# Three separate output banks, a second bank for one Gelu input, and a searched order in an RWKV + Gelu-MLP kernel

## The chip, the cores and the metric

The kernel runs on one core of a Trainium2 chip. The metric is the device time of one execution in microseconds (us), given as the median of several runs. Before the change it is 481.47 us, the median of three runs (480.07, 481.47 and 481.57).

## What is computed

Two stages follow each other in float32. The first is an RWKV recurrence for 4 batches, 8 heads, 768 time steps and head width 48; the second is a Gelu MLP on the 3072 resulting tokens of width 384, with hidden width 2048.

```
cur   = (u * k_t) outer v_t
y_t   = r_t . (state + cur)          # per batch and head; state is 48 x 48
state = w * state + k_t outer v_t    # w is per head and channel, 0.85 to 0.95
x     = y, laid out as 3072 tokens x 384
out   = gelu(x @ w_in) @ w_out       # exact (erf) Gelu
```

## The kernel before, in words

**Tiling.** The 768 time steps are cut into 6 chunks of 128. The 8 heads form 4 pairs, so there are 24 groups (chunk, pair). Inside a group the recurrence is written with powers of w as matrix products: scores of r against k, a masked copy of them, a product with v, and a product with the carried state. The first four groups (chunk 0) have no state to read and are built by `first_group`; the others by `group`. The result of a group is copied out of PSUM as a rounded high half and a low half (`keep`), and together four groups give the x of 512 tokens.

**The MLP** runs over 6 chunks x 16 slices of the hidden width = 96 steps m. In step m `moe1` computes the hidden slice by 9 matmuls (three products: high weights x high x, low weights x high x, high weights x low x, each over three blocks of 128 rows) into the one PSUM bank `Hp`. ScalarE reads `Hp` twice with Gelu (`gh`, rounded, and `gf`, full), and VectorE forms their difference `gl`. `moe2` then adds 9 matmuls into the three output banks, which collect 16 steps. So the next step's first matmul into `Hp` has to wait until both Gelus of the step before have read it. A step is 18 matmuls of 512 columns.

**Weights.** Each of the 16 slices is loaded once as 64-bit numbers (`w_load`, three raw buffers) and turned into a high and a low half by five instructions (`w_split`): two on ScalarE (L395, L398), one add on VectorE (L400), a rounding copy to `wh` on ScalarE (L404), and a subtraction to `wl` on VectorE (L407). All 16 are made during chunk 0 of the MLP.

**PSUM.** The eight banks are `A` (two banks, one tile), `YU` (banks Y and U, one tile), `Hp`, `OO` (output banks 0 and 1, one tile) and `O2`. The chunk-0 groups borrow them: even groups write their scores to `A` and their y to `O2`; odd groups write scores to `OO` and y to `Y`. Two transposes (`flip`) use `U`.

**Order.** All work is given to a planner, the class `Plan`: engine, estimated ns, due time, what it reads and writes by name. `run` carries due times back through the users, `play` then simulates the engines (a free engine takes the ready operation with the smallest due time), and emits each instruction at the moment its turn comes. All DMAs are issued by one queue, SP, in that order, and every engine executes its instructions strictly in that order. Where the simulated TensorE would idle early in the kernel, `play` puts in a dummy matmul ("heat", L305). Semaphores are added afterwards by the framework from what each instruction really touches in a tile.

**The end.** The last chunk's output leaves in four parts (L763 to L774). Then every engine reaches `tc.If` (L909): a general path for values of w outside a range, skipped here; its transfers are issued by ScalarE.

Of the kernel before, what the change touches and what calls it, by code (L numbers as in the profile page):

```python
# [9 lines left out]
F32 = mybir.dt.float32  # L10
# [35 lines left out]
SWAP_DUE = 50000  # L46
ROUND = "a"
# [4 lines left out]
PRODUCT = ("d", "d", "d", "d")  # L52
# [3 lines left out]
class Plan:  # L56
# [11 lines left out]
    def __init__(self, after):  # L68
        self.after = after
        self.ops, self.writer, self.readers, self.reads, self.writes = [], {}, {}, [], []  # L70
        self.heats, self.heat_ns, self.heat_room, self.heat_from, self.heat_to = {}, 0, 0, None, None

# [27 lines left out]
    def run(self):  # L100
        self.users = [[] for _ in self.ops]
        due = [o[2] for o in self.ops]
        for n in reversed(range(len(self.ops))):
# [3 lines left out]
        self.play(due)  # L107

    def play(self, due):

        ops = self.ops
        left = [len(o[4]) for o in ops]
# [4 lines left out]
        clear, unread, held, heating = {}, {}, None, False  # L117
# [3 lines left out]
        for _ in ops:  # L121
# [23 lines left out]
            while e == "pe" and heating:  # L145
# [5 lines left out]
                self.heats[b]()  # L151
# [6 lines left out]
            _, ns, _, fn, _, port = ops[n]  # L158
            if e == "sp":
                free[e] = start + self.DMA_GAP  # L160
                queued = bus - start - self.DMA_LEAD
                bus = max(bus, start + self.DMA_LEAD) + ns / self.DMA_RATES[start >= self.DMA_EARLY]
                end = bus + self.DMA_FIXED + self.DMA_SPREAD * (queued > self.DMA_QUEUED)
# [3 lines left out]
            ins = fn()  # L167
            if port:
                locked[e] = end
                if e == "dve":  # L170
                    held = ins
                elif held is not None:
                    self.after(ins, held, "port")
# [9 lines left out]
            for m in self.users[n]:  # L183
                ready[m] = max(ready[m], end + self.lag(n, m))
                left[m] -= 1
                if not left[m]:
                    heapq.heappush(waiting[ops[m][0]], (ready[m], m))


def rwkv_gelu_mlp(tc, rkT, rkv, wuT, uN, wmlp, r, k, vT, w, u, out):  # L190
    nc = tc.nc
    with ExitStack() as ctx:
# [110 lines left out]

        def heat(dst):
            nc.tensor.matmul(dst, lhsT=zeros[:, 0:128], rhs=zeros, start=True, stop=True)  # L305

        def warm_up():
            for n in range(HEATS):
                heat((A + O + [Y, U])[n % 7])

# [5 lines left out]
        plan.heats, plan.heat_ns, plan.heat_room = {("H",): lambda: heat(Hp), ("U", "Y"): lambda: heat(U)}, HEAT_NS, HEAT_ROOM  # L316
        plan.heat_from = add("pe", 430 * HEATS, 10, warm_up, r=["zeros"], w=["H", "A0", "A1", "O0", "O1", "O2", "Y", "U"])
# [34 lines left out]
        def flip(src):  # L352
            for p in range(NP):
                nc.tensor.transpose(U[:, p * 128:p * 128 + LP], src(p), ident[:LP, :LP])

        def flipped(dst):
            return lambda: nc.scalar.copy(out=dst, in_=U.rearrange("s (p j x) -> s p j x", p=NP, x=64)[:, :, :, :D])

        add("act", 1700, LATER, state_powers, r=["P"], w=["WKs"])
        add("pe", 560, LATER, lambda: flip(lambda p: WKs[:, p, :]), r=["WKs", "ident"], w=["U"])  # L360
        add("act", 400, LATER, flipped(WN), r=["U"], w=["WN"])
# [11 lines left out]
        add("pe", 560, LATER, lambda: flip(lambda p: E[:, p, 1].rearrange("l h i -> l (h i)")), r=EVERY + ["ident"], w=["U"])  # L373
        add("act", 400, LATER, flipped(WN2), r=["U"], w=["WN2"])
# [70 lines left out]
        def first_group(gi, at, XX, XB, y, YB):  # L445
# [8 lines left out]
            for i, e in enumerate(halves):  # L454
# [7 lines left out]
                    r=["P", f"W{p}", f"T{gi}"], w=[f"{TR}{b}" for b in range(bs.start, bs.stop)], port=True)  # L462
            me = PRODUCT[gi]
            mul = nc.vector.tensor_tensor if me == "d" else nc.gpsimd.tensor_tensor
            add("dve" if me == "d" else "pool", dve(512) if me == "d" else pool(512), LATER, lambda: mul(
                out=RK[gi], in0=T[gi][:LP, 0, :, ::-1], in1=T[gi][:LP, 1], op=ALU.mult), r=[f"T{gi}"], w=[f"RK{gi}"], port=True)

            def sum_pairs():
                for b in range(NB):
# [4 lines left out]
            add("pe", 1070, LATER, sum_pairs, r=[f"RK{gi}", "w_sb"], w=["H"])  # L474
            add("act", 110, LATER, lambda: nc.scalar.copy(
                out=sums.rearrange("s (b j) -> s b j", j=2),
                in_=Hp[:, 0:NB * WIDE].rearrange("s (b x) -> s b x", x=WIDE)[:, :, 0:2]), r=["H"], w=[CS])
# [215 lines left out]
        def product1(x, j, n, ks=range(3), start=False, stop=False):  # L693
            wt, a = ((wh, 0), (wl, 0), (wh, 1))[n]
            for k_ in ks:
                nc.tensor.matmul(Hp, lhsT=wt[j][:, 0, k_ * 128:(k_ + 1) * 128], rhs=x[:, a, k_, :],  # L696
# [9 lines left out]
        def moe1(m, at):  # L706
# [6 lines left out]
            n1 = 2 * j  # L713
            if m == 0:
                gaps0 = lambda k_: gaps[2 * k_:2 * k_ + 2]
                for k_ in range(3):
                    first = add("pe", 3 * MM, at + k_, lambda k_=k_: [
                        product1(x, j, n, (k_,), k_ == 0 and n == 0, k_ == 2 and n == 2) for n in range(3)],
                        r=["wh0", "wl0"] + xr("h", (k_,)) + xr("l", (k_,)) + gaps0(k_), w=["H"])
                    plan.heat_to = plan.heat_to or first  # L720
            else:
                for n in range(3):
                    add("pe", 3 * MM, at + n, lambda n=n: product1(x, j, n, start=n == 0, stop=n == 2),
                        r=[f"{('wh', 'wl', 'wh')[n]}{n1}"] + xr("hhl"[n]) + gaps, w=["H"])
            add("act", 480, LATER, lambda: nc.scalar.activation(out=high, in_=Hp, func=AF.Gelu, scale=256.0), r=["H"], w=[GH])  # L725
# [274 lines left out]
```

## Time and profile before

| | |
|---|---|
| median of three runs | 481.47 us |
| the profiled execution | 480.38 us, of which 478.6 us from first to last instruction |
| TensorE matmuls busy | 469.6 us, 98% |
| VectorE, ScalarE, GpSimd busy | 229.0, 181.8, 67.6 us |
| granted TensorE clock | 0.998 of full speed |
| moved by DMA | 46.60 MB, of which 5 to 30 us runs at about 400 GB/s |

PE is TensorE's matmuls, PEld its weight loads, DVE is VectorE, ACT ScalarE, POOL GpSimd, SP the queue that issues the DMAs. L606 is line 606 of the kernel. A matmul's own duration overlaps with its neighbours, so the distance between starts is what counts for the time: a 512-column matmul takes one slot of about 0.233 us. Idle time of an engine that others do not wait for costs nothing.

### The profile page before, as it was taken

The page shows a single profiled execution, that of the slowest core. Times are in us where ns is not written, and L with a number is a line of the kernel's source. Part 1 is how long each engine was busy: PE and PEld are TensorE (multiplying, and loading weights), DVE is VectorE, ACT ScalarE, POOL GpSimd, SP SyncE. Part 2 cuts the span into 40 slices and gives each one's busy share as a digit, 9 for nine tenths or more (in the row PEclk, how much of TensorE's full clock was granted, in tenths as well). Part 3 has the DMA queues.
Part 4 walks back from the last instruction along what each step waited for, and adds up shares of the span by engine and source line. Part 5 has one row for each costly group of instructions (what it writes and reads, how often), then busy time and mean ns, then how long its engine had stood idle before and what let it go on. Part 6 is the DMA issues. An engine that isn't in the chain of part 4 may idle for free.

```text
span 478.6 us, 10284 instructions
## 1 busy us (share of the span) xinstructions
PE 469.6 (98%) x4525; PEld 378.4 (79%) x4525; DVE 229.0 (48%) x345; ACT 181.8 (38%) x333; POOL 67.6 (14%) x91
## 2 busy tenths in 40 slices
PE   8989999999999999999999999999999999999995
PEld 6767788888888787888888888888888887888874
DVE  7989989754354356153543543534434311211111
ACT  9898988232222223232223222223322223322221
POOL 1332021221120222010202202202102000000000
PEclk9999999999999999999999999999999999999999
DMA  8978682314033034031231230321402000100002
GB/s 299 349 305 293 238 296 70 114 54 161 13 95 104 3 113 153 1 105 43 64 105 67 95 102 4 105 59 46 162 29 77 14 0 12 66 1 1 1 0 71
DMA packets 15426, 46.60 MB, mean 97 GB/s; under 512 B 3664, under 2 KB 4048, under 8 KB 15376
## 3 DMA queue, kind: packets, MB, share of 16 engines
q1 hardware_dynamic: 15376, 45.88, 28.9%
q8 instruction: 37, 0.61, 0.5%
q14 instruction: 13, 0.11, 0.1%
HBM read 38.73 MB, written 4.72 MB: 91 GB/s over the span
## 4 chain that ended last, share of the span: by engine, by line
PE 89%; ACT 4%; DMA 4%; DVE 1%; issue 0%; ACTq 0%
PE Hp L696 41%; PE O L737 40%; PE Y L606 2%; DMA E<-W 2%; PE Y L634 2%; PE A L614 2%; DMA raw<-in_wmlp_dram 1%; PE A L623 1%; PE Y L737 1%; ACT wa L395 1%; ACT wh L404 0%; DVE wb L400 0%; ACT W L344 0%; ACT Sa L530 0%; ACT gh L725 0%
## 5 line engine op out<-in xcount | busy, mean ns | idle before, releaser
L696 PE MATMUL Hp<-xx,wh 128*128 128x512 f32 x576 | 168.5, 400 | 0.0
L727 DVE TENSOR_TENSOR gl<-gf,gh 128x512 fp32r<-128x512 f32 x93 | 66.8, 719 | 170.3 <-ACT gf L726 170.0
L725 ACT ACTIVATE gh<-Hp 128x512 fp32r<-128x512 f32 x93 | 55.6, 598 | 219.1 <-PE Hp L696 219.1
L696 PEld LDWEIGHTS Hp<-xx,wh 128*128 128x128 f32 x576 | 105.6, 188 | 25.5 <-ACT gf L726 0.6
L696 PE MATMUL Hp<-xx,wl 128*128 128x512 f32 x288 | 83.0, 395 | 0.0
L737 PE MATMUL O<-gh,wh 128*128 128x512 f32 (+1 forms) x279 | 79.1, 391 | 1.6 <-ACT gh L725 1.5
L737 PE MATMUL O<-gh,wl 128*128 128x512 f32 (+1 forms) x279 | 79.0, 391 | 0.0
L737 PE MATMUL O<-gl,wh 128*128 128x512 f32 (+1 forms) x279 | 78.9, 390 | 0.0
L696 PEld LDWEIGHTS Hp<-xx,wl 128*128 128x128 f32 x288 | 54.1, 188 | 12.9
L737 PEld LDWEIGHTS O<-gh,wh 128*128 128x128 f32 x279 | 52.1, 188 | 15.0 <-ACT gh L725 2.9
L737 PEld LDWEIGHTS O<-gh,wl 128*128 128x128 f32 x279 | 51.6, 188 | 11.7
L737 PEld LDWEIGHTS O<-gl,wh 128*128 128x128 f32 x279 | 51.4, 188 | 11.5 <-issue 0.4
L726 ACT ACTIVATE gf<-Hp 128x512 f32<-128x512 f32 x96 | 56.9, 593 | 0.0
L561 POOL TENSOR_TENSOR Nb<-Nb 128x384 f32<-128x384 f32 x20 | 20.3, 1017 | 125.4 <-DMA Nb<-in_rkv_dram 81.3
L558 DVE TENSOR_TENSOR Tb<-Tb,E 112x1024 f32<-112x1024 f32 x20 | 24.8, 1240 | 2.6 <-DMA Tb<-in_rkT_dram 2.5
L663 DVE SCALAR_TENSOR_TENSOR Sb<-Sa,E,A 48x192 f32<-48x192 f32 x40 | 16.5, 413 | 18.0 <-PE A L623 17.3
L433 ACT CAST xx<-Y 112x512 fp32r<-112x512 f32 (+1 forms) x17 | 10.0, 586 | 39.3 <-PE Y L634 39.3
L564 POOL TENSOR_TENSOR Nb<-Nb,WN 128x384 f32<-128x384 f32 x20 | 20.3, 1017 | 22.9 <-DVE wl L407 14.3
L567 POOL TENSOR_TENSOR Nb<-Nb,u_sb 128x384 f32<-128x384 f32 x20 | 20.3, 1013 | 15.4 <-DVE gl L727 13.6
L570 DVE TENSOR_REDUCE cs<-Nb 128x8 f32<-128x384 f32 x20 | 11.0, 552 | 18.1 <-POOL Nb L567 15.8
L644 POOL MEMSET done<- 1x1 f32 x19 | 1.7, 89 | 125.4 <-PE Y L606 125.4
L670 DVE COPY_PREDICATED Am<-past,A 128x512 f32<-128x512 uint32 x20 | 14.9, 747 | 7.0 <-PE A L623 6.8
(112 smaller groups left out, 376.3 us busy)
## 6 DMA issues: line engine op xcount, KB each, us to landing
raw<-in_wmlp_dram SPq DMA_DIRECT2D x16, 767.8 KB, 6.5
Nb<-in_rkv_dram SPq DMA_DIRECT2D x20, 576.0 KB, 5.5
Tb<-in_rkT_dram SPq DMA_DIRECT2D x20, 512.0 KB, 4.2
out_dram<-raw SPq DMA_DIRECT2D x5, 768.0 KB, 3.6
T<-in_rkT_dram SPq DMA_DIRECT2D x4, 512.0 KB, 5.3
xx<-x SPq DMA_DIRECT2D x30, 64.0 KB, 4.1
N<-in_rkv_dram SPq DMA_DIRECT2D x4, 384.0 KB, 7.3
out_dram<-raw SPq DMA_DIRECT2D x2, 256.0 KB, 2.5
```

Of the source, the lines that this page charges most:

```text
L558: add("dve", 1140, LATER, lambda: nc.vector.tensor_tensor(out=flat, in0=flat, in1=E[:, p, 0].rearrange("l h i -> l (h i)").unsqueeze(1).to ...
L561: add("pool", pool(DM), LATER, lambda: nc.gpsimd.tensor_tensor(out=n[:, 0], in0=n[:, 0], in1=n[:, 1], op=ALU.mult), r=[NK], w=[NR])
L564: add("pool", pool(DM), LATER, lambda: nc.gpsimd.tensor_tensor(out=kn, in0=kn, in1=WN2[:, p].rearrange("s j d -> s (j d)").unsqueeze(1).to ...
L567: add("pool", pool(DM), LATER, lambda: nc.gpsimd.tensor_tensor(out=n[:, 0], in0=n[:, 0], in1=u_sb[:, p, :].unsqueeze(1).to_broadcast([C, N ...
L570: add("dve", 465, LATER, lambda: nc.vector.tensor_reduce(out=sums, in_=n[:, 0].rearrange("s b (j d) -> s (b j) d", d=D), axis=AX.X, op=ALU ...
L663: add("dve", 430, at, lambda l=l, x=x: nc.vector.scalar_tensor_tensor(out=out[quarter(1 - x)], in0=src[l], scalar=E[l, p, 1, h, 32:33], in ...
L670: add("dve", 625, LATER, lambda: nc.vector.copy_predicated(out=am, mask=past2.bitcast(U32).unsqueeze(1).unsqueeze(1).to_broadcast([C, 2, N ...
L696: nc.tensor.matmul(Hp, lhsT=wt[j][:, 0, k_ * 128:(k_ + 1) * 128], rhs=x[:, a, k_, :], start=start and k_ == ks[0], stop=stop and k_ == ks[-1])
L725: add("act", 480, LATER, lambda: nc.scalar.activation(out=high, in_=Hp, func=AF.Gelu, scale=256.0), r=["H"], w=[GH])
L726: add("act", 480, LATER, lambda: nc.scalar.activation(out=gf, in_=Hp, func=AF.Gelu, scale=256.0), r=["H"], w=["gf"])
L727: add("dve", dve(512), LATER, lambda: nc.vector.tensor_tensor(out=low, in0=gf, in1=high.bitcast(F32), op=ALU.subtract), r=["gf", GH], w=[G ...
L737: nc.tensor.matmul(dst[:, a:b], lhsT=wt[j][:, 1, d * 128:(d + 1) * 128], rhs=gt[:, a:b], start=(j == 0 and n == 0), stop=(j == NJ - 1 and ...
```

## The change

Six edits.

1. The output banks 0, 1 and 2 become three tiles of one bank each, in place of one tile of two banks and one of one. Chunk-0 odd groups now write their scores to `YU` and their y to bank O1; the two transposes and one of the dummy-matmul targets move from `U` to O0.
2. The hidden slice of step 1 (and of no other step) is computed into output bank O2 and read by its Gelus from there. The output products of step 0 are split into those for banks 0 and 1 and those for bank 2.
3. `Plan.run` makes 2000 trials: it disturbs the due times of 1 to 4 operations, plays the order up to an operation called the judge (the last hidden product of step 21), replays that order four times with durations disturbed by 4%, and keeps the disturbance where the sum of the four judged times is not larger. The kept due times then give the whole order.
4. The first group's keys and receptances (512 KB) come in two transfers, for batches 0 and 1 and for batches 2 and 3; the product of the two (`RK`) and its sums are split in the same way for this group.
5. In the general path, the transfers move from ScalarE's to GpSimd's queue.
6. `PRODUCT` (all "d", VectorE) goes away.

```diff
+SEARCH, REPLAYS, HEAT, SEED = 2000, 4, 0.0, 2
...
     def run(self):
...
+        noise = [[1 + chance.gauss(0, 0.04) for _ in self.ops] for _ in range(REPLAYS)]
+        judged = lambda order: sum(self.replay(order, x) for x in noise)
+        order = self.play(due, self.judge)
+        end, near = judged(order), [n for n in order if isinstance(n, int) and self.ops[n][0] != "do"]
+        best, kept = end, due
+        for i in range(SEARCH):
+            other = list(due)
+            for n in chance.sample(near, chance.choice((1, 1, 2, 4))):
+                other[n] += chance.gauss(0, chance.choice((1500, 4000, 10000)))
+            got = judged(self.play(other, self.judge))
+            if got <= end + HEAT * REPLAYS * (1 - i / SEARCH) * chance.random():
+                end, due = got, other
+            if end < best:
+                best, kept = end, due
+        due = kept
+        self.issue(self.play(due))
...
-        OO = psp.tile([128, 2, 512], F32, name="O")
-        O = [OO[:, i] for i in range(2)] + [psp.tile([128, 512], F32, name="O2")]
+        O = [psp.tile([128, 512], F32, name=f"O{i}") for i in range(3)]
...
+        halves_of = lambda gi: ((0, 1), (2, 3)) if gi == 0 else (range(NB),)
+
         def load_group(gi, at, r=()):
             s = slot(gi)
-            dma(C * 4096, at, lambda: nc.sync.dma_start(T[s], rkT[gi]), r=r, w=[f"T{s}"])
+            for bs in halves_of(gi):
+                dma(C * 1024 * len(bs), at, lambda bs=slice(bs[0], bs[-1] + 1): nc.sync.dma_start(
+                    T[s][:, :, bs], rkT[gi, :, :, bs]), r=r, w=[f"T{s}{b}" for b in bs] if gi < NP else [f"T{s}"])
...
+            for bs in halves_of(gi):
+                sl, Tn, Rn = slice(bs[0], bs[-1] + 1), [f"T{gi}{b}" for b in bs], [f"RK{gi}{b}" for b in bs]
+                add("dve", dve(128 * len(bs)), LATER, lambda sl=sl: nc.vector.tensor_tensor(
+                    out=RK[gi][:, sl], in0=T[gi][:LP, 0, sl, ::-1], in1=T[gi][:LP, 1, sl], op=ALU.mult),
+                    r=Tn, w=Rn, port=True)
+                add("pe", 268 * len(bs), LATER, lambda bs=bs: sum_pairs(bs), r=Rn + ["w_sb"], w=[f"H{b}" for b in bs])
...
+            dst, H_ = (O[2], "O2") if m == 1 else (Hp, "H")
...
+                    last = add("pe", 3 * MM, at + n, lambda n=n: product1(x, j, n, start=n == 0, stop=n == 2, dst=dst),
+                        r=[f"{('wh', 'wl', 'wh')[n]}{n1}"] + xr("hhl"[n]) + gaps, w=[H_])
+                if m == NJ + 5:
+                    plan.judge = last
...
-            if m < NSTEP - 2:
+            if m == 0:
+                for which in ((0, 1), (2,)):
+                    for n in range(3):
+                        go(m, n, which, at + n)
+            elif m < NSTEP - 2:
...
-            first_group(gi, LATER, AA if even else OO, ["A0", "A1"] if even else ["O0", "O1"],
-                        O[2] if even else Y, "O2" if even else "Y")
+            first_group(gi, LATER, AA if even else YU, ["A0", "A1"] if even else ["Y", "U"],
+                        O[2] if even else O[1], "O2" if even else "O1")
...
-                nc.scalar.dma_start(wb[l, h // 2], w[h].partition_broadcast(D))
+                nc.gpsimd.dma_start(wb[l, h // 2], w[h].partition_broadcast(D))
```

`play` no longer emits; it returns the order, and `issue` emits it. `replay` walks a given order with the disturbed durations and returns the end of the judge.

## Rows read from the trace of the kernel before

**Rows 1.** The page, part 1: busy us (share of the span) xinstructions.
```profile
PE 469.6 (98%) x4525; PEld 378.4 (79%) x4525; DVE 229.0 (48%) x345; ACT 181.8 (38%) x333; POOL 67.6 (14%) x91
```

**Rows 2.** Waits of PE from 20 us on: us in total, times, longest.
```profile
PE O L737 <- ACT gh L725: 1.5, 1, 1.5
PE O L737 <- ACT raw L771: 0.7, 1, 0.7
```

**Rows 3.** Windows: length, busy us by engine, PE clock, DMA share, GB/s.
```profile
5.00:10.00 5.00, 4.92 (x38) 3.61 (x38) 4.56 (x8) 4.90 (x20) 0.00 (x0) 1.00 1.03 409
...
30.00:35.00 5.00, 5.00 (x81) 3.66 (x79) 3.35 (x3) 4.94 (x8) 1.99 (x2) 1.00 0.50 208
40.00:50.00 10.00, 9.88 (x139) 7.75 (x130) 9.89 (x16) 9.89 (x14) 0.09 (x1) 1.00 0.87 302
```

**Rows 4.** Timeline of the last ten us: start, us, engine, line, operation.
```profile
469.91 0.63 PE L737 MATMUL O<-xx,wh 128*128 128x512 f32 x2
470.57 0.60 ACT L771 ACTIVATE raw<-O 128x512 f32<-128x512 f32 x1 [1.93 <-PE O L737]
...
471.22 0.50 PE L737 MATMUL O<-xx,wl 128*128 128x512 f32 x1 [0.69 <-ACT raw L771]
...
474.67 0.52 SPq L774 DMA_DIRECT2D out_dram<-Nb  x1
```

**Rows 5.** Line 909, SP's joins behind the skipped path: ns min/median/max, first to last.
```profile
L909 SPq EVENT_SEMAPHORE  x8: 17/17/17, 475.7 to 477.3; - x8
```

**Rows 6.** Timeline of PE: step 0's last products, its first output products, two later triples.
```profile
26.85 0.40 PE L696 MATMUL Hp<-xx,wh 128*128 128x512 f32 x1
28.73 0.96 PE L737 MATMUL O<-gh,wh 128*128 128x512 f32 x3 [1.48 <-ACT gh L725]
...
46.69 0.86 PE L696 MATMUL Hp<-xx,wl 128*128 128x512 f32 x3
47.39 0.86 PE L696 MATMUL Hp<-xx,wh 128*128 128x512 f32 x3
```

**Rows 7.** Timeline around that wait: weights of step 1, group 4's scaling, first Gelu.
```profile
25.58 1.65 DVE L558 TENSOR_TENSOR Tb<-Tb,E 112x1024 f32<-112x1024 f32 x1
...
26.21 0.81 ACT L404 CAST wh<-wb 128x768 fp32r<-128x768 f32 x1
...
27.16 0.94 DVE L407 TENSOR_TENSOR wl<-wb,wh 128x768 fp32r<-128x768 f32 x1
...
28.09 0.58 ACT L725 ACTIVATE gh<-Hp 128x512 fp32r<-128x512 f32 x1
...
29.80 1.22 DVE L558 TENSOR_TENSOR Tb<-Tb,E 112x1024 f32<-112x1024 f32 x1
```

**Rows 8.** Timeline of the start: key loads, first product, scaled halves, first scores.
```profile
1.28 1.36 SPq L264 DMA_DIRECT2D T<-in_rkT_dram  x3
...
5.44 0.69 DVE L465 TENSOR_TENSOR RK<-T 112x512 f32<-112x512 f32 x1 [0.76 <-DMA T<-in_rkT_dram]
...
7.33 1.22 DVE L459 TENSOR_TENSOR Ts<-T,W 112x512 f32<-112x512 f32 x2
...
8.14 1.18 PE L484 MATMUL A<-Ts 64*128 64x128 f32 x16
```

**Rows 9.** The page, part 6: DMA issues, KB each, median us to landing.
```profile
xx<-x SPq DMA_DIRECT2D x30, 64.0 KB, 4.1
...
out_dram<-raw SPq DMA_DIRECT2D x2, 256.0 KB, 2.5
```

**Rows 10.** Timeline of 41 to 43 us: step 3's low weights and their use.
```profile
41.29 0.95 DVE L407 TENSOR_TENSOR wl<-wb,wh 128x768 fp32r<-128x768 f32 x1
...
42.80 0.86 PE L696 MATMUL Hp<-xx,wl 128*128 128x512 f32 x3
```

**Rows 11.** Timeline before step 32: the last x pieces of chunk 2, its first products.
```profile
170.32 1.63 SPq L441 DMA_DIRECT2D xx<-x  x2
...
179.31 0.97 PE L696 MATMUL Hp<-xx,wh 128*128 128x512 f32 x3
```

More of the change, by code (lines that the diff above doesn't have):

```diff
@@ L100, in run @@
     def run(self):
+        count = len(self.ops)
         self.users = [[] for _ in self.ops]
         due = [o[2] for o in self.ops]
-        for n in reversed(range(len(self.ops))):
+        for n in reversed(range(count)):
             for d in self.ops[n][4]:
@@ new lines, in land, with replay @@
+    def land(self, start, bus, ns, slow=1.0):
+        queued = bus - start - self.DMA_LEAD
+        bus = max(bus, start + self.DMA_LEAD) + ns * slow / self.DMA_RATES[start >= self.DMA_EARLY]
+        return bus + self.DMA_FIXED + self.DMA_SPREAD * (queued > self.DMA_QUEUED), bus
+    def replay(self, order, slow):
+        ops, ends = self.ops, {}
+        free = {e: 800.0 for e in self.LAG}
+        bus, locked, lanes = 0.0, {"dve": 0.0, "pool": 0.0}, [0.0] * self.DMA_LANES
+        for n in order:
+            if not isinstance(n, int):
+                free["pe"] += self.heat_ns
+                continue
+            e, ns, _, _, deps, port = ops[n]
+            start = free[e]
+            for d in deps:
+                start = max(start, ends[d] + self.lag(d, n))
+            if port:
+                start = max(start, locked["pool" if e == "dve" else "dve"])
+            if e == "sp":
+                start = max(start, lanes[0])
+                free[e] = start + self.DMA_GAP
+                ends[n], bus = self.land(start, bus, ns, slow[n])
+                lanes = lanes[1:] + [ends[n]]
+            else:
+                free[e] = ends[n] = start + ns * (slow[n] if e != "pe" else 1.0)
+            if port:
+                locked[e] = ends[n]
+        return ends[n]
@@ L111, in play, with issue @@
+    def issue(self, order):
+        held = None
+        for n in order:
+            if not isinstance(n, int):
+                self.heats[n]()
+                continue
+            ins = self.ops[n][3]()
+            if self.ops[n][5]:
+                if self.ops[n][0] == "dve":
+                    held = ins
+                elif held is not None:
+                    self.after(ins, held, "port")
+    def play(self, due, stop=None):
         ops = self.ops
+        order = []
         left = [len(o[4]) for o in ops]
@@ L187, in play @@
                     heapq.heappush(waiting[ops[m][0]], (ready[m], m))
+            if n == stop:
+                break
+        return order
 def rwkv_gelu_mlp(tc, rkT, rkv, wuT, uN, wmlp, r, k, vT, w, u, out):
@@ L301, in rwkv_gelu_mlp @@
         add("act", 520, LATER, spread_ones, r=["ident", "zeros"], w=["spread"])
+        HB = [f"H{b}" for b in range(NB)]
         def heat(dst):
@@ L461, in first_group, with sum_pairs @@
                         in1=W[:, p, 0:C].unsqueeze(1).unsqueeze(1).to_broadcast([LP, 2, nb, C]), op=ALU.mult),
[L462 to L469, printed above, removed]
+                    r=["P", f"W{p}"] + [f"T{gi}{b}" for b in range(bs.start, bs.stop)],
+                    w=[f"{TR}{b}" for b in range(bs.start, bs.stop)], port=True)
+            def sum_pairs(bs):
+                for b in bs:
                     nc.tensor.matmul(
```

73 lines of the change are left out of this document (32 added, 41 removed).

## The prediction

> **What bounds the kernel now.** I read the page first. TensorE's matmuls are busy for 469.6 us, 98% of the span, and no other engine passes half of it [rows 1]. Busy matmuls overlap, so this alone does not say that no time is left; the list of PE's waits does. From 20 us on it has two entries: 1.5 us for the first Gelu of step 0, and 0.7 us for a copy of the output at the very end [rows 2]. In between, a triple of 512-column matmuls starts 0.70 us after the one before it [rows 6], 0.233 us per matmul, and this goes on for 96 steps. Nothing in the change removes a matmul or makes one faster. It can therefore gain in three places only: at the end, in the 1.5 us wait, and in the start-up before it. What is saved there shifts the whole dense stretch, one for one, as long as the other engines can follow.
>
> Whether they can is read from the windows. At 5 to 10 us DVE is busy for 4.56 of 5 us, ACT for 4.90, PE for 4.92 and the DMA engines all the time at 409 GB/s; at 40 to 50 us DVE and ACT are busy for 9.89 of 10 each. Only 30 to 35 us has room, with DVE at 3.35 of 5 [rows 3]. So start-up is a stage with four full resources, and up to about 60 us the weights arrive just in time.
>
> **Three output tiles: the end.** In the last us PE runs the products for bank 0, then those for bank 1. ScalarE's copy of bank 0 starts at 470.57, behind the second matmul of the pair that starts at 469.91, which already belongs to bank 1; and PE's next matmul into bank 1 starts at 471.22 and is put down to that copy [rows 4]. The two touch different banks but one tile, so both waits come from the tile. Without it the next matmul would start two slots after 469.91, at 470.38, and not at 471.22: 0.84 us. Behind it only the last products, a copy and the last output transfer follow (SP issues it at 474.67), all in one chain, so the end moves by the same amount. I take -0.84. Ends: nothing, if another wait stands there (ScalarE's copy lasts to 471.17), and -0.84.
>
> **General path on GpSimd.** The path is skipped, so no transfer of it runs. What remains is the join: SP executes eight semaphore instructions at L909, from 475.7 to 477.3, as the last output transfers land [rows 5]. If these belong to the lanes that ScalarE's skipped transfers would use, they change or go; they hold 8 x 17 ns of work and some distance between each. I take -0.2; the ends are -0.5, about the distance of six of them (1.6 us over seven steps), and +0.2 if GpSimd's lanes are added to the list.
>
> **Step 1 in the third bank.** Step 0's last hidden product starts at 26.85, so its slot ends at 27.08; PE then stands until 28.73, because the first thing in its queue is an output product that needs `gh` of step 0 [rows 6], and `gh` itself starts at 28.09 [rows 7]. Into `Hp` nothing may be written until both Gelus have read it. In O2 it may: nine products of step 1, 2.1 us, can follow at once, and they cover the 1.65 us. They need both halves of step 1's weights. The high half is done at 27.02, in time. The low half runs from 27.16 to 28.10 [rows 7], and the fourth product wants it at 27.78. With the order as it is, three products (0.70 us) go at once and the other six wait a little; with an order that puts group 4's scaling (25.58, 1.65 us) behind the subtraction, all go. That scaling may wait, since group 4 is due only after the output products. Ends: -0.70 and -1.65; I take -1.4, nearer to the second, as a reordering is part of the change. What the split of step 0's output products adds is a wait of three of them (bank 2) for step 1's Gelus; six others and step 1's own work stand ahead.
>
> **First keys in two transfers.** DVE's first product waits 0.76 us for the 512 KB of T0 and starts at 5.44 [rows 8]. DVE is full from there on, so a start that is earlier by x is worth up to x in start-up. With the second half the queue gets one more issue: three T issues take 1.36 us [rows 8], 0.46 each, and every later load is issued that much later; since the engines move 409 GB/s from 5 us on [rows 3], the loads behind are queued in any case and most of that is hidden. Does a half really release its half? Writes into parts of one SBUF tile are told apart: the scores of batches 0 and 1 start at 8.14, while the second of the two scaling instructions, which writes the other batches of the same tile, runs until 8.55 [rows 8].
>
> The Trainium skill speaks against this edit: SBUF — State Buffer, section "The DMA setup-cost knee", has a roughly fixed 2 us per transfer and asks for the largest single transfer when DMA bounds. The trace's queue holds many transfers in flight at once, so I do not add that cost to the sum; what it would do is the fourth case below.
>
> **The searched order.** The search can only move what DVE, ACT and POOL do before about 127 us. The most that I can read for it is a DVE operation stretched by a concurrent GpSimd one: group 4's scaling takes 1.65 us where the next takes 1.22 [rows 7], 0.43. Together with the 0.76 the start-up ends earlier by at most 1.2; the least is a loss of 0.46, the issue. I take -0.7, nearest to the wait of 0.76.
>
> **What is late next.** With 2.1 us gained before step 1 ends, step 3 asks for its low weights earlier: they are done at 42.24 and used at 42.80 [rows 10], a slack of 0.56. The rest must come out of the 1.65 us that DVE idles between 30 and 35 us [rows 3], and an order that is looked for anew can use it. I put +0.4 for what is not recovered; ends 0 and +1.5 (2.1 less 0.56).
>
> **Sum.** -0.84 - 0.2 - 1.4 - 0.7 + 0.4 = -2.74. The profiled execution took 480.38 us, 478.6 of span and 1.8 around it, so 477.64. It lies 1.1 below the median of 481.47; the three runs lie at 480.07, 481.47 and 481.57, in two places, and the changed kernel will have its own two. I add half of the distance, 0.55: 478.2.
>
> **The rivals.** A difference of 0.3% (1.4 us) is about what runs of this kernel can tell from none.
>
> 1. *The weights take it back.* Steps 3 to 7 find DVE full, and only the 0.56 us of slack survives: -0.84 - 0.2 - 0.56 = -1.6, with the 0.55 479.3. For it: DVE and ACT at 9.89 of 10 [rows 3]. Against: DVE's idle 1.65 us just before.
> 2. *The search finds everything:* -0.84 - 0.5 - 1.65 - 1.2 = -4.2, which gives 476.7. Against: four full resources at 5 to 10 us [rows 3].
> 3. *Slower, through the judge.* The search counts time only up to step 21. What it pushes behind that point looks free to it, the groups of chunk 2 above all, whose x step 32 needs. Before, the last pieces of that x are issued from 170.32 to 171.95 [rows 11] and land 4.1 us later [rows 9], at about 175.5 by the last issue; step 32 starts at 179.31 [rows 11]. So 3.8 us of delay are free and every us beyond stalls PE. It decides the sign from a delay of 3.8 + 2.7 = 6.5 us; at 9 us the time is 478.2 + 5.2 = 483.4. Against: the groups form a row in which each waits for the one before, and those behind step 21 keep their due times.
> 4. *The halves cost a transfer of their own.* If the second half were served only after the first, with the 2.5 us that a 256 KB transfer takes [rows 9] each, T0 would be complete 5.0 us after its issue at 1.28, at 6.28, 0.84 later than now. The start-up term turns from -0.7 to +0.84: 479.7. Against: the queue at 409 GB/s. This is the page's rule, as a mechanism of this kernel.
> 5. *The banks don't come apart:* semaphores may still tie them, then the 0.84 at the end stays and the time is 479.0.
>
> **How the numbers follow.** Forecast (476.9 to 479.5) 0.52, rival 1 0.20, rival 2 0.11, rival 3 0.08, rival 4 0.05, rival 5 0.04. The range takes in all but most of rival 3 and the outermost of rival 2: 476.0 to 480.9. Faster by over 0.3% means below 480.0: the forecast with 0.49, two thirds of rival 1 (0.14), rival 2, and 0.06 of the last two, together 0.80, from which I take 0.03 because the 1.4 us of two places in the runs can hide a gain of 1.6. So 0.77 faster, 0.15 within 0.3%, 0.08 slower.
>
> **What would show it.** In the changed profile: no wait of PE for L771 and the last DMA issue some 0.8 us earlier relative to the last hidden product; matmuls of step 1 into O directly behind step 0's, with no stop of 1.5 us; step 0's last product before 26.5; and groups of 18 matmuls at 0.233 from about 43 us. The rivals show as PE waiting for `wl` or `wh` between 33 and 60 us (1), as a stop before step 32 (3), as T0's second half landing after 6 us (4), as the old wait at the end (5). I am wrong if start-up ends later than now or if the dense stretch has new holes.

## The result, and the profile after

The change makes the kernel slower: 484.55 us, median of 8 runs (483.08 to 487.89), against 480.34 for the kernel before beside it (8 runs, 479.77 to 481.57); ratio 1.0084, 95% interval 1.0061 to 1.0106, about +4.0 us. The forecast was 478.2, at the most 480.9. The profiled execution took 485.07 us, 483.6 of it from first to last instruction, 5.0 more than before.

The page of the changed kernel, beside [rows 1]; in its last line each digit is a fortieth of the span, 12 us, in tenths of the full clock:

```profile
span 483.6 us, 10304 instructions
...
PE 473.3 (98%) x4524; PEld 382.3 (79%) x4524; DVE 227.5 (47%) x346; ACT 182.1 (38%) x333; POOL 68.7 (14%) x91
...
PEclk9699999999999999999999999999999999999998
```

PE is "busy" for 3.7 us more with the same products to make: in the second slice its clock is low. Windows beside [rows 3] (length, busy us of PE, PEld, DVE, ACT, POOL, granted clock, DMA share, GB/s) place it:

```profile
5.00:10.00 5.00, 3.73 (x26) 3.07 (x26) 2.74 (x6) 4.52 (x20) 0.00 (x0) 1.00 0.87 250
10.00:15.00 5.00, 3.53 (x21) 2.98 (x18) 4.25 (x6) 1.72 (x7) 0.00 (x0) 0.51 1.03 417
15.00:20.00 5.00, 5.00 (x38) 4.58 (x39) 4.44 (x5) 3.57 (x13) 1.73 (x2) 0.50 1.02 389
```

At 5 to 10 us the DMA engines move 250 GB/s where they moved 409, DVE works 2.74 us where it worked 4.56, and from 10 to 20 us TensorE has half its clock (1.2 of 2.4 GHz). The first MLP matmul comes at 30.85 us; before it came at 23.83:

```profile
30.85 0.50 PE L766 MATMUL Hp<-xx,wh 128*128 128x512 f32 x1
```

```profile
23.83 0.50 PE L696 MATMUL Hp<-xx,wh 128*128 128x512 f32 x1
```

The end is as forecast. Beside [rows 4]: ScalarE copies bank 0 while PE goes on in bank 1, with no wait:

```profile
475.98 0.63 PE L810 MATMUL O<-xx,wh 128*128 128x512 f32 x2
476.42 0.60 ACT L848 ACTIVATE raw<-O 128x512 f32<-128x512 f32 x1 [1.72 <-PE O L810]
476.45 0.40 PE L810 MATMUL O<-xx,wl 128*128 128x512 f32 x1
```

So the loss is all in start-up. The list below gives how much later the second Gelu of step n starts than before (us, from the timelines of the profiled executions). Up to step 24 the orders differ in what else PE has done by then, so only the last columns count as time. Each line is one execution; e1's took 483.55 us, 3.3 above the median of its runs, the others lie within 0.6 of theirs. From step 33 on all lines are flat: nothing happens in the dense stretch.

```
step                           0      1      4     12     21     24     33     95
changed                     6.74   4.94   4.47   5.89   4.08   5.97   6.05   6.05
e2 no search                3.94   2.10   5.06   4.63   4.64   4.64   4.61   4.62
e1 one load, searched       4.04   3.48   3.26   4.52   2.70   4.60   4.43   4.43
e3 whole, no search         0.39  -1.45  -0.25  -0.19  -0.19  -0.19  -0.01  -0.01
e8 as e3, path on ScalarE  -0.05  -1.90  -0.68  -0.61  -0.60  -0.60  -0.64  -0.62
e15 as e3, w2 earlier       0.86  -0.94  -0.46  -0.90  -0.90  -0.90  -0.87  -0.86
e18 as e1, one moved        1.38  -0.27  -0.88   0.67  -1.15   0.75   0.65   0.67
```

**How the loss is made.** DVE's products and scalings of the first keys, beside [rows 8]:

```profile
4.87 0.42 DVE L541 TENSOR_TENSOR RK<-T 112x256 f32<-112x256 f32 x1 [0.39 <-DMA T<-in_rkT_dram]
6.85 0.42 DVE L541 TENSOR_TENSOR RK<-T 112x256 f32<-112x256 f32 x1 [1.56 <-DMA T<-in_rkT_dram]
...
10.14 0.69 DVE L541 TENSOR_TENSOR RK<-T 112x512 f32<-112x512 f32 x1 [0.85 <-DMA T<-in_rkT_dram]
11.44 0.69 DVE L541 TENSOR_TENSOR RK<-T 112x512 f32<-112x512 f32 x1 [0.60 <-DMA T<-in_rkT_dram]
...
12.92 1.16 DVE L528 TENSOR_TENSOR Ts<-T,W 112x1024 f32<-112x1024 f32 x1
```

T0 is the load of the first keys, "T1" the load behind it. T0's first half lands at 4.85, only 0.57 before the whole T0 did (5.42), the second at 6.83, and T1 at 10.12 where it had landed at 6.67. In the searched order the products of T1 and of the load behind it (10.14, 11.44) both stand ahead of the next scaling (12.92). And lateness is handed on: SP has eight loads under way at a time, so each load is issued when the eighth before it has landed. The second weight load is issued when T1 has landed; it is the eleventh load behind the third in the kernel before, the twelfth behind the fourth in the changed one. In the kernel before:

```profile
6.68 0.33 SPq L380 DMA_DIRECT2D raw<-in_wmlp_dram  x1
```

In the changed kernel, with the next one:

```profile
10.14 0.33 SPq L449 DMA_DIRECT2D raw<-in_wmlp_dram  x1
11.43 0.33 SPq L330 DMA_DIRECT2D Tb<-in_rkT_dram  x1
```

The second weight load lands at 21.21 (before 17.40), the third at 30.98 (before 25.23). This trace is the latest of five with these loads: in e7, e9, e14 and e17 below, T1 lands at 8.91 to 9.77 and the third weights at 28.96 to 29.79. A landing from one trace is thus good to about 1 us with the split; In the ten traces with T0 whole and T1 issued right behind it, T1 lands at 6.5 to 7.1. ScalarE in the changed kernel stands for that third one (needed in step 2), with the last cast of x and step 1's high weights behind it in its queue:

```profile
31.00 0.90 ACT L467 ACTIVATE wb<-raw 128x768 int32<-128x768 uint32 x1 [1.57 <-DMA raw<-in_wmlp_dram]
31.81 0.57 ACT L502 CAST xx<-O 128x512 fp32r<-128x512 f32 x1
32.27 0.83 ACT L473 CAST wh<-wb 128x768 fp32r<-128x768 f32 x1
```

PE stands for that cast before step 1's first product:

```profile
33.16 0.97 PE L766 MATMUL O<-xx,wh 128*128 128x512 f32 x3 [0.65 <-ACT wh L473]
```

### The profile page after: what moved, and what is told of

It is laid out like the page before. It is cut to its first block, busy times and chain, and to the rows that moved or that the text cites. A ratio compares the mean times of both kernels' runs of the same rounds, so it can differ in the third digit from the quotient of the medians.

```text
span 483.6 us, 10304 instructions
## 1 busy us (share of the span) xinstructions
PE 473.3 (98%) x4524; PEld 382.3 (79%) x4524; DVE 227.5 (47%) x346; ACT 182.1 (38%) x333; POOL 68.7 (14%) x91
## 4 chain that ended last, share of the span: by engine, by line
PE 85%; DVE 5%; DMA 5%; SPq 3%; ACT 1%; issue 0%
PE Hp L766 39%; PE O L810 38%; PE Y L676 2%; DMA T<-in_rkT_dram 2%; PE A L684 2%; PE Y L704 2%; DMA raw<-in_wmlp_dram 2%; DVE wb L469 1%; PE A L693 1%; DVE wl L476 1%; PE Y L810 1%; DMA Nb<-in_rkv_dram 1%; SPq L435 1%; DVE gl L800 1%; SPq L330 0%
## 5 line engine op out<-in xcount | busy, mean ns | idle before, releaser
L766 PE MATMUL Hp<-xx,wh 128*128 128x512 f32 x570 | 166.8, 400 | 0.0
L800 DVE TENSOR_TENSOR gl<-gf,gh 128x512 fp32r<-128x512 f32 x93 | 65.8, 707 | 167.1 <-ACT gf L799 163.5
L766 PEld LDWEIGHTS Hp<-xx,wh 128*128 128x128 f32 x570 | 104.3, 188 | 25.4 <-ACT gf L799 1.2
L637 POOL TENSOR_TENSOR Nb<-Nb,u_sb 128x384 f32<-128x384 f32 x20 | 21.5, 1075 | 24.0 <-DVE gl L800 13.5
L502 ACT CAST xx<-Y 112x512 fp32r<-112x512 f32 x15 | 8.8, 587 | 35.1 <-PE Y L704 35.0
L464 ACT ACTIVATE wa<-raw 128x768 f16<-128x768 bf16 x16 | 17.5, 1094 | 2.1 <-DVE wb L469 2.1
```

The costliest lines, as they stand in the source:

```text
L464: add("act", 930, LATER, lambda: nc.scalar.activation(out=a.bitcast(F16).rearrange("p (n t) -> p n t", t=2)[:, :, 1], in_=top.bitcast(BF16 ...
L637: add("pool", pool(DM), LATER, lambda: nc.gpsimd.tensor_tensor(out=n[:, 0], in0=n[:, 0], in1=u_sb[:, p, :].unsqueeze(1).to_broadcast([C, N ...
L766: nc.tensor.matmul(dst, lhsT=wt[j][:, 0, k_ * 128:(k_ + 1) * 128], rhs=x[:, a, k_, :], start=start and k_ == ks[0], stop=stop and k_ == ks ...
L800: add("dve", dve(512), LATER, lambda: nc.vector.tensor_tensor(out=low, in0=gf, in1=high.bitcast(F32), op=ALU.subtract), r=["gf", GH], w=[G ...
```

## The experiments

Ratios are to the runs of the kernel before on the same chip, so they need not be the quotient of the medians shown; 0.001 is 0.48 us. Landings are those of one trace each.

| run | T0 | order | T1 landed | third weights landed | median us | ratio (95%) |
|---|---|---|---|---|---|---|
| before | whole | planner | 6.67 | 25.23 | 480.34 | 1 |
| changed | 2 x, 1 KB rows | searched | 10.12 | 30.98 | 484.55 | 1.0084 (1.0061 to 1.0106) |
| e1 | whole | the changed one | 6.63 | 27.49 | 480.25 | 0.9999 (0.9973 to 1.0024) |
| e2 | 2 x, 1 KB rows | planner | 10.04 | 29.19 | 483.58 | 1.0052 (1.0033 to 1.0072) |
| e3 | whole | planner | 6.78 | 25.64 | 478.63 | 0.9952 (0.9932 to 0.9973) |
| e4 | whole | searched anew | 6.57 | 25.31 | 480.39 | 0.9982 (0.9965 to 1.0000) |
| e5 | 2 x, 4 KB rows | planner | 8.32 | 27.67 | 482.16 | 1.0022 (1.0003 to 1.0041) |
| e6 | 1 x, 1 KB rows | planner | 8.18 | 27.03 | 480.01 | 0.9986 (0.9975 to 0.9998) |
| e13 | 2 x, 2 KB rows | planner | 7.91 | 26.20 | 480.31 | 0.9988 (0.9975 to 1.0002) |

**e1 to e4: the split and the search, each alone.** e1 keeps the changed order and moves T0 at once:

```diff
+                def load(bs=slice(bs[0], bs[-1] + 1)):
+                    if bs.start == 0:
+                        return nc.sync.dma_start(T[s], rkT[gi])
```

> The changed kernel with T0 loaded by one transfer, in the place of the first of the two; every engine keeps the changed kernel's order. Before took 480.3, the change 484.5. Theory L (the two transfers of 1 KB rows land late, T0's second half at 6.83 and T1 at 10.12): T0 lands near 5.4 again, T1 near 6.7, the first MLP matmul falls from 30.85 to about 24, and the time to 478 to 479.5. Theory O (the order that the search wrote is what stalls: DVE has keys of two later T loads ahead of the scalings of T1): T0 lands near 5.4, but DVE still waits for the two later loads, the first MLP matmul stays behind 28 and the time at 482.5 to 484.5.

```diff
-SEARCH, REPLAYS, HEAT, SEED = 2000, 4, 0.0, 2
+SEARCH, REPLAYS, HEAT, SEED = 0, 4, 0.0, 2
```

> The changed kernel without the search: T0 still in two transfers, the start-up order is the planner's own. Theory L: T0's second half lands behind 6 again, T1 behind 9, and the time stays at 482 to 484.5. Theory O: the loads may be late, but nothing waits in a false place behind them; the first MLP matmul comes at 24 to 26 and the time is 478 to 480.5.

e3 takes this edit and the next; e4 the next alone:

```diff
-        halves_of = lambda gi: ((0, 1), (2, 3)) if gi == 0 else (range(NB),)
+        halves_of = lambda gi: (range(NB),)
```

> Three output tiles, step 1 in the third and the general path's transfers on GpSimd; T0 whole and no search, so that start-up is practically that of before. Theories L and O expect the same here: start-up as before (first MLP matmul within 0.5 of 23.83), the 1.5 us wait behind step 0 gone or cut to 0.3 at most, the wait for the output copy gone: 480.3 - 0.84 - (0.7 to 1.65) = 477.8 to 478.8. A third theory, S (the tiles or the skipped path on GpSimd cost something all over the program), expects 480.5 or more.

> The changed kernel with T0 whole in the planner too, so that the search writes a new order for it. Theory L: at most the time of the same kernel without search, 477.5 to 478.8, as the search can only help once the loads land early. Theory O: the search again ties the in-order queues to load times that the chip does not keep: 480 or more, with DVE waits over 1 us for a T load before 15 us.

Neither L nor O alone. The split costs 0.0100 without search (e3 to e2, 4.8 us) and 0.0085 with it (e1 to changed, 4.1). The search costs 0.0047 with T0 whole (e3 to e1) and 0.0030 when it writes a new order for that (e3 to e4). What is left without both is the gain that was forecast for the rest: -0.0048, 2.3 us. e4 missed O's sign: no DVE wait of over 1 us for a T load before 15 us, and still slower than no search. e3 missed one forecast of its own: the 1.5 us stop should have gone or shrunk to 0.3, and 0.67 us of it is left (below).

The granted clock does not explain either difference away. In five of e2's twelve executions it was 0.998 or more, as in all seven of e3; those five took 480.90 to 483.12 us, e3's 478.52 to 479.65. In e4 it was 0.998 or more throughout, and its fastest execution (479.88) is slower than e3's slowest. In e1 it does matter; see e18.

**e5, e6, e13: what in the split costs.** Base is e3; only T0's transfer differs (below, in the order e5, e6, e13):

```diff
+                        nc.sync.dma_start(T[s][0:64], rkT[gi, 0:64])
+                        return nc.sync.dma_start(T[s][64:128], rkT[gi, 64:128])
...
+                        short = lambda t: t.rearrange("p a (h b) x -> p (a h) (b x)", h=2)[:, ::-1]
+                        return nc.sync.dma_start(short(T[s]), short(rkT[gi]))
...
+                        nc.sync.dma_start(T[s][:, 0], rkT[gi, :, 0])
+                        return nc.sync.dma_start(T[s][:, 1], rkT[gi, :, 1])
```

> Like the run with T0 whole and no search (478.63; T0 landed 5.52, T1 6.78), but T0 in two transfers of 64 partitions with rows of 4 KB. Theory N (it is the second transfer that costs): the second half lands behind 6.5, T1 behind 8.5, and the time is 481 or more. Theory R (it is the rows of 1 KB that cost): both halves are in by 5.9, T1 by 7.2, and the time is 478.4 to 479.3.

> Like the run with T0 whole and no search, but the one transfer of T0 moves rows of 1 KB (four per partition, taken in reverse order, so that they don't merge into one of 4 KB; the keys and gains of T0 therefore come out in changed places). Theory R: T0 lands at 7 to 8, T1 at 8.5 to 10, and the time is 481 to 484. Theory N: T0 lands at 5.4 to 5.8 as with long rows, and the time is 478.4 to 479.3.

> T0 in two transfers over all 128 partitions with rows of 2 KB, the rest as in the run with T0 whole and no search (478.63, T1 landed 6.78). Two transfers with 4 KB rows over 64 partitions each had T1 at 8.32 (482.16), one with 1 KB rows at 8.18 (480.01). If a second transfer costs by itself, T1 lands at 8.0 to 8.8 and the time is 480.3 to 482.5. If it was that only 64 partitions were read at a time, T1 lands by 7.5 and the time is 478.6 to 479.6.

Each of N and R holds in part: both costs are there, but e6's time lies between the two forecasts, and e5 is just short of N's landings. T1 is read from SP's second weight load, which waits for it; in e5, e6, e13:

```profile
8.34 0.33 SPq L453 DMA_DIRECT2D raw<-in_wmlp_dram  x1
```

```profile
8.20 0.33 SPq L453 DMA_DIRECT2D raw<-in_wmlp_dram  x1
```

```profile
7.93 0.33 SPq L453 DMA_DIRECT2D raw<-in_wmlp_dram  x1
```

Against e3's 6.78, a second transfer alone delays T1 by 1.1 (e13) to 1.5 us (e5), short rows alone by 1.4, both by 3.3 (e2; 2.1 to 3.3 in the five other traces with both). These three are one trace each: that each part delays T1 is clear, which of them delays it more is not. In e13 both halves were in at 5.01, before e3's whole T0 (5.52), and it is still 1.7 us slower than e3: what counts here is the load behind, not the half that comes early.

**e7, e9, e14: the granted clock.** Dummy matmuls ahead of the PE work that had waited: 4 before the first scores, 6 before T1's sums (e7), and 13 before step 1's first product, into bank O1 (e9) or U (e14).

```diff
+                for _ in range(4 if gi == 0 and bs[0] == 0 else 0):
+                    heat(U)
...
+                for _ in range(6 if gi == 1 else 0):
+                    heat(U)
...
-product1(x, j, n, start=n == 0, stop=n == 2, dst=dst),
+[heat(U) for _ in range(13 if m == 1 and n == 0 else 0)] and None or product1(x, j, n, start=n == 0, stop=n == 2, dst=dst),
```

> The changed kernel with ten more idle-filling 512-column matmuls into a bank that nobody reads: four ahead of the first scores and six ahead of T1's sums, where PE stood 0.95 and 1.47 us. Theory C (the granted clock, 0.51 from 10 to 20 us, is a cost of its own): the clock stays at 1.00 there, the sums that took 2.00 take 1.13 again, the first MLP matmul falls from 30.85 to 27 to 28.5 and the time from 484.5 to 481 to 482.5. Theory D (the late loads and DVE's order set the pace, PE's clock is hidden behind them): the clock rises, the first MLP matmul stays behind 30 and the time within 0.8 of 484.5.

> The kernel with the ten filling matmuls (484.35; first MLP matmul at 26.35, then PE stood 3.12 us at step 1's first product until its weights were there, and the clock fell to 0.55 in 30 to 35 and 0.77 in 35 to 40) with 13 more filling matmuls in front of that product. Theory W (the weights' landing sets the pace up to step 1; the clock costs only where PE is dense): step 1 starts no earlier than 31, but the clock stays at 1.00 in 30 to 40, which gives 5 x 0.45 + 5 x 0.23 = 3.4 us back: 480.8 to 482. Theory V (behind step 1 the weights still set the pace, so that the clock is hidden there too): 483.8 to 484.8.

> The ten filling matmuls again and 13 more ahead of step 1's first product, now into a bank that is free by then (in the run before they stood 2.9 us themselves, for a bank that was still read, and then lay on the path). Theory W (the clock costs where PE is dense): the 13 end before the weights are there (28.0 + 3.0 = 31.0), the clock stays at 1.00 in 30 to 38, and the time falls from 484.35 to 481 to 482.5. Theory V (weights set the pace behind step 1 too): 483.8 to 484.8.

e7: 484.35 us, ratio 1.0068 (1.0053 to 1.0084). Its windows and PE's longest wait:

```profile
10.00:15.00 5.00, 5.00 (x45) 4.22 (x46) 4.82 (x6) 3.29 (x13) 0.00 (x0) 1.00 1.03 419
15.00:20.00 5.00, 4.90 (x59) 3.93 (x53) 5.00 (x7) 4.97 (x16) 2.95 (x3) 1.00 1.09 350
...
30.00:35.00 5.00, 3.87 (x9) 3.10 (x10) 2.89 (x3) 4.29 (x8) 1.01 (x1) 0.55 0.82 306
```

```profile
PE O L770 <- ACT wh L473: 3.1, 1, 3.1
```

The clock stayed up, the first MLP matmul came 4.5 us earlier (26.35), and the median moved by no more than runs differ: PE reached step 1 early, stood 3.1 us for its weights, and the clock fell there. Not all of the 4.5 us is the clock's, as T1 landed 1.2 us earlier in this trace than in the changed kernel's. Both theories missed half: C the time, D the first matmul. e9 says nothing of the clock: its 13 matmuls waited 2.9 us themselves, for O1, and then lay on the path (488.48 us, 1.0153). e14 is the cleanest one (its fillers end about 0.3 us behind step 1's high weights): PE's waits from 5 us on are 0.3 us in all,

```profile
PE Hp L537 <- DVE RK L543: 0.3, 1, 0.3
```

the clock is 1.00 throughout, and it takes 483.30 us, 1.0058 (1.0038 to 1.0078): about 1.2 us of the 4.0, between W and V, with intervals that overlap. A count by PE's own time had misled: the half-speed stretch (T1's sums 2.00 us in place of 1.13, and so on up to 20 us) adds up to 3.8 us, but by e7 and e14 most of it would have been a wait for weights.

**e17, e18: why the searched order costs.** The one ScalarE instruction shown above at 31.00 goes behind step 1's high weights, in the changed kernel (e17) and in e1 (e18):

```diff
-        self.issue(self.play(due))
+        order = self.play(due)
+        find = lambda x: next(n for n in order if isinstance(n, int) and self.ops[n][0] == "act" and x in self.writes[n])
+        early, late = find("wb2"), find("wh2")
+        order.remove(early)
+        order.insert(order.index(late) + 1, early)
+        self.issue(order)
```

> The changed kernel with one instruction of ScalarE moved: the conversion that waits for the third weight load (its wait of 1.57 us ends at 31.00) stands behind the last x cast and step 1's high weights, which it had in front of it in the queue. Nothing else is moved. Theory A (ScalarE's place in the order ties step 1 to the third load): PE's wait of 0.65 us for the high weights goes and step 1's products start by 32.6 in place of 33.16; 483.0 to 484.2. Theory B (the loads are late and the clock low, ScalarE's order adds nothing): 484.3 to 485.

> The same move in the kernel with the searched order and T0 in one transfer (480.25; there ScalarE stood 4.08 us at this instruction and PE 3.01 behind it, and in 4 of 12 runs a low clock followed). Theory A: PE's wait falls below 0.7 us, step 1 starts 2 to 3 us earlier; Gelu of step 0 still stands behind the moved instruction, so 1 to 2 us of it reach the end: 478.2 to 479.4, and no run above 482. Theory B: 480 to 480.6 and PE's wait moves to Gelu.

e1's ScalarE and PE without the move:

```profile
27.51 0.89 ACT L469 ACTIVATE wb<-raw 128x768 int32<-128x768 uint32 x1 [4.08 <-DMA raw<-in_wmlp_dram]
28.30 0.57 ACT L504 CAST xx<-O 128x512 fp32r<-128x512 f32 x1
28.76 0.84 ACT L475 CAST wh<-wb 128x768 fp32r<-128x768 f32 x1
```

```profile
29.66 1.65 PE L768 MATMUL O<-xx,wh 128*128 128x512 f32 x3 [3.01 <-ACT wh L475]
```

With it (e18), step 1 follows step 0's products; what is left waits for Gelu:

```profile
26.77 0.86 PE L773 MATMUL O<-xx,wh 128*128 128x512 f32 x3
...
31.06 0.73 PE L817 MATMUL O<-gh,wh 128*128 128x512 f32 x2 [1.33 <-ACT gh L805]
```

e18 takes 479.06 us, 0.9968 (0.9952 to 0.9984) against e1's 0.9999; e17 483.38, 1.0055 (1.0042 to 1.0069) against 1.0084. One place in one queue is worth 1.4 and 1.5 us: in e1 some two thirds of what the search cost. The intervals overlap a little, but the two pairs agree, both times lie in A's ranges, and PE's wait for `wh` is gone in both. Theory A, then.

How the move gives so much back in e1 is seen in its executions. The lines of e1 above come from one of four in which the granted clock was 0.990 to 0.995 over the whole run (483.07 to 485.16 us): behind PE's stop of 3.01 us it stands at 0.50 from 30 to 35 us. In the other eight it was 0.998 or more, and they average 479.7 us; e18's twelve, all at 0.998 or more, average 479.3. So most of the 1.5 us is that the clock no longer falls behind the stop; some half a us is left for the stop itself. In e17 the clock still falls (0.70 from 10 to 15 us, 0.61 from 15 to 20, in the changed kernel 0.51 and 0.50), and how its 1.4 us divide is open.

**e10 to e12: the search held in.** e10 lets it disturb all engines but SP, e11 judges at step 40, e12 does both; T0 whole.

```diff
-        end, near = judged(order), [n for n in order if isinstance(n, int) and self.ops[n][0] != "do"]
+        end, near = judged(order), [n for n in order if isinstance(n, int) and self.ops[n][0] not in ("do", "sp")]
...
-                if m == NJ + 5:
+                if m == 2 * NJ + 8:
```

> T0 whole; the search may move what DVE, ACT and GpSimd do, but not the due times of the loads: SP's order is that of the unsearched kernel (478.63). Theory Q (the searched order costs by the order of the loads): the third weight transfer lands at 25.2 to 25.8 and the time is 477.5 to 478.7. Theory E (it costs by the engines' order): as with the full search, 479.8 to 480.6.

> T0 whole, full search as in the run that took 480.39, but the search judges at step 40 in place of step 21. There step 21 was 0.17 behind the kernel of before and step 24 0.81: 0.64 of what the judge counted had only been put behind it. Theory J (the judge's place is what costs): the difference between step 21 and 24 goes, and the time is 479.2 to 479.8. Theory M (the order follows load times that the chip does not keep, wherever it is judged): 480 or more.

> Both: the loads keep their due times, and the search of the other engines is judged at step 40. If the unsearched order leaves something that such a search finds, 477.3 to 478.3; if the loads set the pace whatever the engines' order, 478.3 to 479.

e10: 480.33 us, 0.9983 (0.9965 to 1.0001), with the loads' order of e3, so Q falls: the engines' order costs by itself (in its trace PE stands 2.1 us for the transfer into `E`, with the clock at 0.66 from 20 to 25 us). Here too most of the cost goes with the clock: its four executions at 0.998 or more took 478.75 to 479.36, about as e3's, the other eight 480.03 to 481.48. e11: 482.47, 1.0037 (1.0017 to 1.0056): J falls, a later judge is no cure. e12: 479.88, 0.9978 (0.9960 to 0.9996), above both of its ranges. No searched order reached e3's.

**e8, e15, e16: the parts that gain.** e8 is e3 with the general path on ScalarE; e15 and e16 are e3 with the third weight load issued earlier.

```diff
-                nc.gpsimd.dma_start(...)
+                nc.scalar.dma_start(...)
...
-LOADS = (1, 2, 3, "w0", "w1", 4, "u", "w2", 5)
+e15: LOADS = (1, 2, 3, "w0", "w1", "w2", 4, "u", 5)
+e16: LOADS = (1, 2, 3, "w0", "w1", 4, "w2", "u", 5)
```

> Like the run with T0 whole and no search (478.63), but the general path's skipped transfers are issued by ScalarE again. If GpSimd's path shortened the join (span's end 1.03 behind the last landing, before 1.47) and lengthened the start (first memset at 0.54, before 0.30), then the join goes back to about 1.45, the first memset to 0.30, and the two nearly cancel: 478.6 to 479.0. If neither belongs to the path, both stay and the time is 478.6.

> T0 whole and no search (478.63), with the third weight load ahead of the loads of group 4 and of u. There step 1 ran 1.45 ahead of before and step 10 level with it. If the third weights' landing takes the 1.45 back, it lands at 23 to 24 in place of 25.64, more than half of the 1.45 is still there at step 48, and the time is 477.4 to 478.3. If group 4 (its keys 1.9 us later) or DVE takes it, 478.5 to 480.

> As the run before, but the third weight load stands behind group 4 and ahead of u alone. The weights land 0.3 to 0.7 earlier than 25.64, group 4 stays in time: 478.0 to 478.6; no difference (478.6) if DVE sets the pace.

e8: 479.15 us, 0.9967 (0.9954 to 0.9980). The first memset is back at 0.31 us (e3 and the changed kernel 0.54), the whole dense stretch 0.6 earlier than in e3, and SP has its joins again, which e3 lacks:

```profile
L986 SPq EVENT_SEMAPHORE  x8: 17/17/17, 473.8 to 475.8; - x8
```

Its span ends 1.5 us behind the last landing, e3's 1.1. GpSimd's path thus gains 0.4 us at the end and loses 0.23 at the start; the runs' net, 0.7 us for it, is not settled: the intervals overlap. e15: 478.13 us, 0.9949 (0.9931 to 0.9967), third weights in at 21.66, 4.0 us before e3's, and 0.86 us ahead at step 95, where e3 is 0.01 ahead. PE's longest wait from 5 us on is 0.2 us, where e3 and e8 stand 0.67 for step 1's Gelu: here step 2's first products fill that place, as their weights are ready. It is the fastest of all, but by ratio only 0.0003 below e3, which these runs can't tell from nothing. e16: 479.18, 0.9962 (0.9949 to 0.9975), no gain, and the trap of e17 and e18 again, here in the planner's own order: ScalarE waits for the third weights with step 1's high half (27.14) behind, and PE stands 1.55 us for that.

```profile
24.92 1.09 ACT L464 ACTIVATE wa<-raw 128x768 f16<-128x768 bf16 x1 [1.42 <-DMA raw<-in_wmlp_dram]
25.88 0.56 ACT L502 CAST xx<-O 128x512 fp32r<-128x512 f32 x1
26.34 0.90 ACT L467 ACTIVATE wb<-raw 128x768 int32<-128x768 uint32 x1
27.14 0.81 ACT L473 CAST wh<-wb 128x768 fp32r<-128x768 f32 x1
```

## Why the prediction was wrong, step by step

**Three output tiles (-0.84): right.** No wait is left at the end. In e3 the matmul that started at 471.22 [rows 4] starts at 470.38, as worked out; the pair before it stands where it stood (469.92), and PE's last one comes 0.88 earlier.

**General path (-0.2): right in size, partly by luck.** The joins on SP go, which takes 0.4 us off the end, and the start comes 0.23 later, a term that the sum did not have. The two make -0.2 in the traces (e8, e3); the runs give -0.7, not settled.

**Step 1 in the third bank (-1.4) and what is late next (+0.4): a wait that was named and put at nothing.** The stop of 1.48 us goes, and step 1's hidden products do follow step 0's at once. But then PE stands for the three products of step 0 that go to bank 2, until step 1's second Gelu has read that bank. In e8:

```profile
31.75 0.50 PE L810 MATMUL O<-gh,wh 128*128 128x512 f32 x1 [0.67 <-ACT gf L799]
```

e3 stands there for 0.67 us too. The prediction names this wait and gives it no price, because "six others and step 1's own work stand ahead"; these were through 0.67 us too soon. The 1.90 us by which step 1's Gelu is ahead in e8 is not a gain of that size: PE has made step 1's hidden products ahead of step 0's output products. Once both are made, at 32.64 where the kernel before is at 34.05 with three more products (0.70 us) done, PE is 0.7 ahead, and 0.62 of it is there at step 95. So next to nothing is taken back behind it: e8 has no wait of PE for weights from 33 us on. In place of -1.4 + 0.4 = -1.0 stand about -0.6. Rival 1 left 0.56 of this gain, close to what came, but through steps 3 to 7 waiting for weights, which they did not. Without the start-up term the sum was -2.04, and e3 measures about -2.3: with a step 1 that is worth less and a path that may be worth more, part of this agreement is luck.

**First keys in two transfers, with the searched order (-0.7, ends -1.2 and +0.46): the step that failed.** The second transfer was priced by SP's issue, 0.46, "and most of that is hidden" because the queue is full from 5 us on [rows 3]. That was read from a stretch in which all transfers were whole. With the split the engines move 250 GB/s there, T1 lands 3.45 us later, and a full queue hides nothing: eight under way, so each late landing is a late issue, down to the third weights (+5.75 with the searched order, +3.96 in e2 without it). Where the sum had a gain of 0.7, e2 and e3 put the split at +4.8, and the search adds to it. Rival 4 had the right mechanism, the second half behind 6 us (6.83 came), with 0.05 and the wrong price: it followed T0 and not the load behind it. The Trainium skill (SBUF — State Buffer, section "The DMA setup-cost knee") asks for the largest single transfer, because each pays a roughly fixed 2 us. The runs agree that the second transfer costs; what they show is another quantity, 1.1 to 1.5 us (e13, e5) by which the load behind lands later.

**The searched order** was taken as harmless at the worst: it may only move. But every engine executes in order, and where the order puts an instruction that waits for a load ahead of work due sooner, a late load stalls both. e17 and e18 show one such place. It costs 1.4 to 2.3 us with T0 whole (e4, e1); that all of this comes from load times that the chip does not keep is not shown, as e10, with the loads' due times left alone, costs as much. Rival 3 had the wrong place for it: nothing stalls at step 32 or behind.

## What to carry to other kernels

A first transfer that is split so that work can begin earlier has to be priced at the load behind it, and where a fixed number of loads is under way at a time, at every load after that; look whether the half really lands earlier, and how long its rows become. A searched order is only as good as the times that it was searched with: look in each in-order queue for an instruction that waits for a transfer while something due sooner stands behind it. When an engine shows a low clock, look where: from 10 to 20 us, behind late loads, filling the idle time gave back little (e7, e14); in e1, behind a stop just ahead of the dense stretch, the executions with a low clock took some 4 us more on average. And price a bank that is lent out for the wait until it is read.

## What the runs showed of the hardware

Half of T0 over 64 partitions with 4 KB rows landed at 5.44 us, 3.9 after its issue; the whole, with twice the bytes, at 5.52, 4.0 after (e5, e3). Transfers with 1 KB rows or 64 partitions held SP for 0.58 to 0.78 us each, a whole T0 and 2 KB rows for 0.40 to 0.43. Why 1 KB rows delay the next load by 1.4 us is open. TensorE's clock fell to its lower level (1.2 GHz) at PE's stops of 3.0 and 3.1 us in e1 and e7, and stayed at 2.4 GHz over one of 2.9 us in e9; in the changed kernel it fell from 10 us on with no stop longer than 0.95 us between 5 and 10 us. The length of one stop thus does not tell, and no run here gives the rule. In e1, one program, the 8 runs at a granted clock of 0.998 or more took 478.50 to 480.38 us, the 4 at 0.990 to 0.995 took 483.07 to 485.16.
